# FFT convolution: the second half of the second tile's pixels loaded behind ScalarE's first copy

## The chip, the cores and the metric

The kernel runs on one core of one Trainium2 chip. The metric is the device time of one execution in microseconds, as the median of several runs. A separate profiled execution gives the trace that the views below come from.

## The reference

The reference is a circular 7x7 convolution, written as a product of two-dimensional Fourier transforms over height and width:

```
Xf = rfft2(x, axes=(1, 2))            # x: 1 x 224 x 224 x 96
Wf = rfft2(pad(w to 224 x 224))       # w: 7 x 7 x 96 x 96
Yf = einsum('bhwi,hwio->bhwo', Xf, Wf)
y  = irfft2(Yf, axes=(1, 2))          # bf16, 1 x 224 x 224 x 96
```

## The kernel before

The kernel transforms along the height only. The 224 rows are eight blocks of 28 rows; each block with 6 rows of overlap is taken to 17 frequencies (numbered s). Along the width the convolution stays direct, with the even and the odd columns combined so that fewer products are needed.

The width is cut into seven tiles of 32 columns (numbered t). The pixels of a tile come in two halves (numbered jg): half 0 holds the upper 112 image rows and half 1 the lower 112, each with 6 rows of overlap above. `load_rows` (line 177) loads a half with two DMAs on SP's queue: 112 rows of 6 KB (672 KB), then the 6 rows of overlap (36 KB). Tile 0 lies in `x0_bufs`, all later tiles in `xn_bufs` (xn0 and xn1, one for each half). `load_x(t, jg)` (line 188) loads a half of a tile.

The work has four kinds of steps, and TensorE does the products of each:

- Pixels to frequencies: matmuls of pixel columns with the matrix Fm (in the views: MATMUL pb<-Fm,xn), copied by ScalarE or VectorE from PSUM to xf. For tile 1 these are the jobs of `f_jobs` (line 535).
- Filters to frequencies: matmuls on the loaded filters wq, copied to WF (`wide_jobs`, `prep_jobs`).
- Product rounds, `b_round(t, s, ...)` (line 589): matmuls over the 96 channels for one tile and one frequency (MATMUL pb<-WF,xf and pb<-WF,J; J holds differences of xf made by VectorE). Their sums go to yf and, every few rounds, by DMA to scr in DRAM.
- Frequencies back to pixels: scr is loaded with another layout (tt), multiplied with G and put out.

At the start SP issues all loads in one sequence (lines 210 to 217): filters, tile 0's two halves with their left borders, the second copy of the filters, then both halves of tile 1. An in-order queue carries these issues.

The product rounds of tile 0 and tile 1 are interleaved by the loop at line 848. In each round, `mid()` and `end()` call jobs of other steps between the matmuls of the round, paced by steps: a queue with `add(a, b, jobs)` is spread over steps a to b - 1, two steps a round. The jobs of tile 1's first part are added at r == 1 with steps 4 to 7, that is, in the rounds r = 2 and 3. There are eight, four for half 0 and then four for half 1. Each has eight matmuls. The middle of round 2 takes three, its end three, and the middle of round 3 two. So half 0 is first read in the middle of round 2 and half 1 at its end.

In a round at the lowest and highest frequency (`if s in REAL`, line 616), ScalarE copies the first bank of products from PSUM to a temporary tile (line 619) before the second bank's products are made. For t = s = 0 this is ScalarE's first instruction of the product rounds.

The instructions of an engine follow the order in which the program names them; a helper records most of them, so that they all have line 98 in the views.

Of the kernel before, what the change touches and what calls it, by code (L numbers as in the profile page):

```python
# [63 lines left out]
def kernel(  # L64
# [7 lines left out]
    _, H, W, C = x.shape  # L72
# [12 lines left out]
    SYNC = mybir.DependencyInfo(mybir.DependencyClass.Sync, mybir.DependencyReason.DATA)  # L85
# [19 lines left out]
    VE, SE, GE, TE, DE = (_Ordered(e) for e in (nc.vector, nc.scalar, nc.gpsimd, nc.tensor, nc.sync))  # L105
# [9 lines left out]
    def bank():  # L115
        return pools["psb"].tile([128, 512], F32, name="pb")
# [60 lines left out]
    def load_rows(xb, jg, w0, npx):  # L177
        h0 = jg * HB - PAD
        n = npx * C

        def ld(p0, p1, hh):
            return dma(xb[p0:p1, 0:n], x[0, hh:hh + (p1 - p0), w0:w0 + npx, :].rearrange("h w c -> h (w c)"))
        return ld(PAD, R, h0 + PAD), ld(0, PAD, h0 % H)

    def xbuf(t, jg):
        return (xn_bufs if t else x0_bufs)[jg]

    def load_x(t, jg):
        return load_rows(xbuf(t, jg), jg, t * 2 * TW, 2 * TW)
# [13 lines left out]
    def load_copy(p, h):  # L203
        n = (C * C, WC)[h]
        for i in range(3):
            load_w(p, 0, PW - 1, h, i * n // 3, (i + 1) * n // 3)
            if i == 1:
                load_last(p + PW - 1, h)
# [4 lines left out]
        load_rows(xh_bufs[jg], jg, W - PAD, PAD)  # L213
    load_x(0, 1)
    load_copy(K1, 1)
    for jg in range(2):
        load_x(1, jg)

    wu = cpool.tile([128, 128], BF16, name="wu")
    wur = wu[:].unsqueeze(1).to_broadcast([128, 4, 128])  # L220
# [364 lines left out]
        ]  # L585

    yf_cur = {}

    def b_round(t, s, mid, end, ydve=False, planes=()):
        xf = xf_tiles[t][0:C]  # L590
# [22 lines left out]
        b0, b1 = bank(), bank()  # L613
        merge = t < 2 and s in MERGE
        tt_ = tv_pool.tile([128, 4 * C], F32, name="tt_")
        if s in REAL:
            for part in range(2):
                conv(b0, part * C, 0, part)
            SE.copy(out=tt_[:, 0:2 * C], in_=b0[:, 0:2 * C])
            mid()  # L620
            for mi, m in enumerate((2, 1)):
                for part in range(2):
                    conv(b1, (mi * 2 + part) * C, m, part)
            VE.tensor_tensor(out=yv.rearrange("p r m o -> p m r o"),
                             in0=tt_[:, 0:2 * C].rearrange("p (r o) -> p r o", o=C).unsqueeze(1).to_broadcast([128, 2, 2, C]),
                             in1=b1[:, 0:4 * C].rearrange("p (m r o) -> p m r o", m=2, r=2), op=ALU.add)
            load["a"] += 110 + 0.9 * 192
            load["v"] += 540
            for f in planes:
                f()  # L630
            end()
        else:
            v = tv_pool.tile([128, 2, 2, C], F32, name="v")
            if merge:
                conv(b0, 2 * C, 0, 0, both=True)
                conv(b0, 2 * C, 2, 0, add=True)
                conv(b0, 3 * C, 1, 0, add=True)
                conv(b0, 0, 0, 1)
                conv(b0, C, 0, 2)
                SE.mul(out=tt_[:], in_=b0[:, 0:4 * C], mul=-0.5)  # L640
                u, pr = tt_[:, 2 * C:4 * C].rearrange("p (m o) -> p m o", m=2), tt_[:, 0:2 * C]
            else:
                for part in range(3):
                    conv(b0, part * C, 0, part)
                conv(b0, 3 * C, 2, 0)
                conv(b0, 4 * C, 1, 0)
                u = tv_pool.tile([128, 2, C], F32, name="u")
                SE.mul(out=tt_[:, 0:3 * C], in_=b0[:, 0:3 * C], mul=-0.5)
                pr = tt_[:, C:3 * C]
            if puts:  # L650
                puts.pop(0)()
            if not merge:
                VE.scalar_tensor_tensor(out=u[:], in0=b0[:, 3 * C:5 * C].rearrange("p (m o) -> p m o", m=2), scalar=-0.5,
                                        in1=tt_[:, 0:C].unsqueeze(1).to_broadcast([128, 2, C]), op0=ALU.mult, op1=ALU.add)
            mid()
            for mi, m in enumerate((2, 1)):
                for pi, part in enumerate((1, 2)):
                    conv(b1, (mi * 2 + pi) * C, m, part)
            VE.scalar_tensor_tensor(out=v.rearrange("p m r o -> p m (r o)"),
                                    in0=pr.unsqueeze(1).to_broadcast([128, 2, 2 * C]), scalar=-2.0,  # L660
                                    in1=b1[:, 0:4 * C].rearrange("p (m q) -> p m q", m=2), op0=ALU.mult, op1=ALU.add)
            def ysum(eng):
                return eng.tensor_tensor(out=yv.rearrange("p r m o -> p m r o"), in0=v[:],
                                         in1=u.unsqueeze(2).to_broadcast([128, 2, 2, C]), op=ALU.add)
            if ydve:
                ysum(VE)
            last = None
            for f in planes:
                last = f()
            if not ydve:  # L670
                y = ysum(GE)
                if len(planes) > 1:
                    tc.add_manual_dep(y.ins, last.ins.name, SYNC, reason="sum after planes")
            load["a"] += 490 if merge else 410
            load["v"] += (560 if ydve else 250 if t < 2 else 0) + (560 if merge else 900)
            end()
# [103 lines left out]
    held = [0, 0]  # L780
# [34 lines left out]
    def pace(q, k):  # L815
        a, b, jobs, n = q
        if k < a:
            return
        due = n if k >= b - 1 else -(-n * (k - a + 1) // (b - a))
        while jobs and n - len(jobs) < due:  # L820
            jobs.pop(0)()

    def fills(qs, k):
        def f():
            for q in qs:
                pace(q, k)
        return f
# [20 lines left out]
    for r in range(NS + LAG):  # L848
        if r == 0:
            for i in range(1, PGRP[0][1]):  # L850
                add(max(2 * i - 3, 0), 2 * i - 1, [diff(i)])
            for i in range(N5, REAL[1]):
                add(2 * i - 2, 2 * i, [diff(i)])
            add(0, 4, fj[1][0] + fj[1][1])
            add(8, 12, fj[2][0] + fj[2][1])
        if r == 2:
            new_xf(1, SH2[0], SH2[1])
        for p in range(3):
            if r == (1, 3, 6)[p]:
                if p:  # L860
                    new_xf(1, SH2[p], SH2[p + 1])
                else:
                    xf_tiles[1] = xf_bufs[1]
                fj = f_jobs(1, p)
                if p == 2:
                    for jg in range(2):
                        fj[jg][-1] = then_load(fj[jg][-1], 2, jg)
                add((4, 7, 12)[p], (7, 11, 15)[p], fj[0] + fj[1])
        for p in range(3):
            if r == SH2[p + 1] + 1 - (p == 2):  # L870
                new_xf(2, SH2[p], SH2[p + 1])
                fj = f_jobs(2, p)
                if p == 2:
                    for jg in range(2):
                        fj[jg][-1] = then_load(fj[jg][-1], 3, jg)
                add(2 * r, 2 * r + (8, 7, 5)[p], fj[0] + fj[1])
        if r == PGRP[-2][1] + 1:
            assert not any(q[2] for q in qs[:len(PGRP) - 1])
            wtmp_cm.__exit__(None, None, None)
            t_pool = ctx.enter_context(tc.tile_pool(name="tt", bufs=NTT, side="right"))  # L880
            t2_pool = ctx.enter_context(tc.tile_pool(name="tt2", bufs=1, side="right"))
            yo_pool = ctx.enter_context(tc.tile_pool(name="yo", bufs=2, side="right"))
            g_pool = ctx.enter_context(tc.tile_pool(name="gp", bufs=1, side="right"))
            GA = g_pool.tile([KA, 4 * B], BF16, name="GA")
            GB = g_pool.tile([128, 2, 4 * B], BF16, name="GB")
            GE.memset(GA[:], 0.0)
            GE.memset(GB[:], 0.0)
        if r == 3:
            g_fin()
        if r == NS + 3:  # L890
            queue_c(0)
        for t in range(2):
            s = r - LAG * t
            if not 0 <= s < NS:
                continue
            now = bursts.pop((r, t), ())
            now = jit(*now) if now else []
            now, rest = rest + now[:2], now[2:]
            both = LAG <= r < NS
            b_round(t, s, fills(qs, 2 * r + (t if both else 0)), fills(qs, 2 * r + (t if both else 1)), False, now)  # L900
    assert not rest and not bursts and nburst == 2 * len(JGB)
    if NP2:
        ps0_cm.__exit__(None, None, None)
# [109 lines left out]
```

## Time and profile before

| what | value |
|---|---|
| median of 3 runs | 268.43 us (266.54 to 268.81) |
| profiled execution: its own time | 267.37 us |
| its span (first to last instruction) | 265.7 us |
| mean granted clock of TensorE | 0.995 |
| busy: TensorE matmuls | 252.3 us |
| busy: VectorE | 216.2 us |
| busy: ScalarE | 198.1 us |
| busy: GpSimd | 98.5 us |
| moved by DMA | 46.78 MB, mean 176 GB/s |

PE is TensorE's matmul side and PEld its weight loads, which overlap the matmuls. DVE is VectorE, ACT ScalarE, POOL GpSimd, and SPq the queue on which SyncE issues DMAs. The busy times are sums over the whole span; they tell which engine is close to the span but not where a wait lies. Times in a timeline are counted from the start of the span. In a timeline row the bracket gives how long the engine stood idle before the row and what ended that.

### The profile page before, as it was taken

To read this page: it belongs to the slowest core of one execution; us is meant where nothing else is said; L and a number is where in the kernel's file an instruction comes from. 1 tells how busy PE (TensorE), PEld (TensorE's weight loads), DVE (VectorE), ACT (ScalarE), POOL (GpSimd) and SP (SyncE) were. 2 spreads that over 40 slices of the span, in tenths; PEclk is the share of its full clock that TensorE was granted. 3 is DMA by queue.
4 is the path that set the end of the run, shared out by engine and by line. 5 is a ranking of instruction groups with operands and counts; after the bars stand their busy time and mean duration, and the time that the engine had idled before them with its cause. 6 is when DMAs were issued, how large, how long until landed. Compare 5 with 4: busy or idle time off the path is not lost.

```text
span 265.7 us, 12114 instructions
## 1 busy us (share of the span) xinstructions
PE 252.3 (95%) x5121; PEld 234.6 (88%) x5121; DVE 216.2 (81%) x459; ACT 198.1 (75%) x475; POOL 98.5 (37%) x152
## 2 busy tenths in 40 slices
PE   7987999999999999999999999999999999999993
PEld 2976999999999999999999998989999889879861
DVE  6887999899999689778887788878888889978523
ACT  8987978688854678988988799976987764287123
POOL 7782234645556442322223413333124323432100
PEclk9999999999999999999999999999999999999998
DMA  7994104511111797978785587989588533897846
GB/s 181 276 187 114 47 4 143 171 47 47 49 48 73 211 245 180 294 221 243 230 215 181 143 247 213 243 229 352 188 155 240 175 122 129 201 246 192 247 122 192
DMA packets 46946, 46.78 MB, mean 176 GB/s; under 512 B 35356, under 2 KB 38120, under 8 KB 46892
## 3 DMA queue, kind: packets, MB, share of 16 engines
q1 hardware_dynamic: 44604, 43.95, 59.3%
q10 hardware_dynamic: 2288, 2.06, 2.4%
q8 instruction: 40, 0.66, 1.1%
q14 instruction: 14, 0.11, 0.1%
HBM read 24.66 MB, written 21.33 MB: 173 GB/s over the span
## 4 chain that ended last, share of the span: by engine, by line
PE 73%; DMA 13%; DVE 8%; issue 2%; ACT 1%; SPq 1%; ACTq 0%; DVEq 0%
PE pb L98 72%; DVE J L98 3%; DMA WF<-in_x_dram 3%; DMA xf<-scra 2%; DMA tt<-scr 2%; DVE v L98 2%; DVE WF L98 2%; DMA wq<-in_w_dram 2%; DMA scrb<-yf 1%; DMA scra<-yf 1%; DMA xf<-scrb 1%; SPq L98 1%; DVE yf L98 1%; DVE u L98 1%; PE ps L98 1%
## 5 line engine op out<-in xcount | busy, mean ns | idle before, releaser
L98 PE MATMUL pb<-WF,J 96*128 96x96 bf16 x2821 | 163.0, 206 | 1.9 <-DVE J L98 1.3
L98 PEld LDWEIGHTS <-J 96*128 96x128 bf16 x2821 | 138.1, 98 | 12.6 <-issue 3.9
L98 POOL TENSOR_TENSOR yf<-v,u 128x384 bf16<-128x384 f32 x79 | 81.6, 1045 | 143.7 <-issue 85.5
L98 ACT CAST xf<-pb 96x408 bf16<-96x408 f32 (+4 forms) x140 | 65.8, 489 | 7.8 <-PE pb L98 4.4
L98 PE MATMUL pb<-WF,xf 96*128 96x96 bf16 x952 | 60.0, 206 | 0.9 <-DVE J L98 0.9
L98 DVE TENSOR_TENSOR J<-xf 96x456 bf16<-96x456 bf16 (+3 forms) x85 | 56.3, 702 | 0.0
L98 PEld LDWEIGHTS <-xf 96*128 96x128 bf16 x952 | 47.2, 98 | 1.1 <-ACT xf L98 0.8
L98 PE MATMUL pb<-Fm,xn 118*128 118x136 bf16 (+3 forms) x640 | 45.5, 199 | 1.9 <-issue 1.8
L98 PE MATMUL pb<-tt,Gm 102*84 102x384 bf16 (+1 forms) x132 | 32.8, 326 | 0.7 <-DVE u L98 0.4
L98 PEld LDWEIGHTS <-xn 118*128 118x128 bf16 x640 | 30.2, 97 | 2.2 <-issue 2.2
L98 ACT CAST J<-pb 84x384 bf16<-84x384 f32 (+1 forms) x65 | 28.0, 489 | 2.6 <-PE pb L98 2.3
L98 ACT CAST yo<-pb 84x384 bf16<-84x384 f32 (+1 forms) x63 | 27.1, 486 | 2.3 <-POOL yf L98 1.3
L98 DVE TENSOR_TENSOR J<-J 96x912 bf16<-96x912 bf16 (+2 forms) x42 | 24.1, 573 | 0.0
L98 ACT CAST WF<-pb 96x480 bf16<-96x480 f32 x42 | 21.1, 561 | 0.3 <-PE pb L98 0.3
L98 PEld LDWEIGHTS <-wq 128*128 128x128 bf16 (+1 forms) x288 | 19.7, 149 | 1.5 <-ACT wq L98 1.5
L98 DVE TENSOR_TENSOR yf<-v,u 128x384 bf16<-128x384 f32 x26 | 14.9, 572 | 0.9
L98 PE MATMUL pb<-wq 128*128 128x120 bf16 x192 | 15.2, 224 | 0.0
L98 DVE TENSOR_TENSOR WF<-WF 96x960 bf16<-96x960 bf16 x15 | 13.6, 905 | 1.4 <-ACT WF L98 1.3
L98 PEld LDWEIGHTS <-Gm 102*84 102x84 bf16 (+1 forms) x132 | 11.1, 117 | 1.0 <-issue 0.3
L98 ACT COPY xf<-xf 96x816 bf16<-96x816 bf16 (+3 forms) x20 | 11.1, 607 | 0.0
L98 PEld LDWEIGHTS <-wu 128*112 128x112 bf16 (+1 forms) x52 | 6.5, 127 | 4.8 <-issue 1.7
L98 ACT CAST tt<-pb 112x384 bf16<-112x384 f32 x8 | 3.6, 480 | 9.2 <-PE pb L98 9.0
(397 smaller groups left out, 255.7 us busy)
## 6 DMA issues: line engine op xcount, KB each, us to landing
scr<-yf SPq DMA_DIRECT2D x30, 288.0 KB
xn<-in_x_dram SPq DMA_DIRECT2D x12, 672.0 KB
tt<-scr SPq DMA_DIRECT2D x24, 336.0 KB
out_dram<-yo SPq DMA_DIRECT2D x12, 252.0 KB
out_dram<-J SPq DMA_DIRECT2D x12, 252.0 KB
tt<-scr SPq DMA_DIRECT2D x6, 288.0 KB
WF<-in_x_dram SPq DMA_DIRECT2D x2, 672.0 KB
out_dram<-tt SPq DMA_DIRECT2D x8, 168.0 KB
```

Source lines behind the costliest of these rows:

```text
L98: r = fn(*a, **k)
```

## The change

Half 1 of tile 1 is no longer issued at the start. Its two DMAs are issued after the first product round has been written down in the program, and the first of them gets a dependency on the copy that ScalarE makes in that round. SP's queue keeps the same order of DMAs, as nothing else is issued on it in between; the first of the two now waits on a semaphore of ScalarE. No other engine's order changes.

```
-    for jg in range(2):
-        load_x(1, jg)
+    load_x(1, 0)
...
+    held_x = None
...
-            SE.copy(out=tt_[:, 0:2 * C], in_=b0[:, 0:2 * C])
+            held = SE.copy(out=tt_[:, 0:2 * C], in_=b0[:, 0:2 * C])
+            if t == s == 0:
+                nonlocal held_x
+                held_x = held
...
             b_round(t, s, fills(qs, 2 * r + (t if both else 0)), fills(qs, 2 * r + (t if both else 1)), False, now)
+            if r == 0:
+                for d in load_x(1, 1):
+                    tc.add_manual_dep(d.ins, held_x.ins.name, SYNC, reason="second half behind the first products")
```

## The prediction

> **What bounds the kernel now.** I read the page first: parts 1 and 4 for the engine that sets the end, part 3 for what the queues carry.
>
> ```profile
> span 265.7 us, 12114 instructions
> PE 252.3 (95%) x5121; PEld 234.6 (88%) x5121; DVE 216.2 (81%) x459; ACT 198.1 (75%) x475; POOL 98.5 (37%) x152
> ...
> q1 hardware_dynamic: 44604, 43.95, 59.3%
> ...
> q8 instruction: 40, 0.66, 1.1%
> ...
> PE 73%; DMA 13%; DVE 8%; issue 2%; ACT 1%; SPq 1%; ACTq 0%; DVEq 0%
> ```
>
> TensorE is busy for 95% of the span and carries 73% of the chain. Time is saved or lost only where PE stands still. Queue q8 is of use below: 40 packets and 0.66 MB are 16 KB each, and PE runs 5121 + 5121 = 10242 instructions, 256 for each packet. I read q8 as PE's instruction refill.
>
> Second, the timeline of PE around the tile whose load is moved (start, length, instructions, and in brackets the idle time before).
>
> ```profile
> 21.79 0.94 PE L98 MATMUL pb<-wq 128*128 128x120 bf16 x12
> 22.89 0.39 PE L98 MATMUL pb<-Fm,xn 118*128 118x64 bf16 x8 [0.16 <-ACT xf L98]
> 25.08 0.64 PE L98 MATMUL pb<-Fm,xn 118*128 118x64 bf16 x16 [1.79 <-issue]
> 25.55 0.76 PE L98 MATMUL pb<-WF,J 96*128 96x96 bf16 x14
> 26.15 0.66 PE L98 MATMUL pb<-wq 128*128 128x120 bf16 x8
> 26.65 0.86 PE L98 MATMUL pb<-Fm,xn 118*128 118x64 bf16 x24
> ```
>
> The 1.79 us is the longest idle time of PE after its start-up. "issue" means that no semaphore ended it, and the weight load that leads the group (25.07, 1.91 us idle) waits for none. The first 8 + 16 of these matmuls read xn0 (first half), and so do 8 of the 24 at 26.65; the first one on xn1 (second half) starts at 26.88.
>
> Third, the timelines of SP's queue and of ScalarE.
>
> ```profile
> 9.42 2.63 SPq L98 DMA_DIRECT2D wq<-in_w_dram  x5
> 12.10 4.04 SPq L98 DMA_DIRECT2D xn<-in_x_dram  x4
> 28.33 0.36 SPq L98 DMA_DIRECT2D scr<-yf  x1
> ...
> 17.57 0.32 ACT L98 COPY tt__482<-pb 128x192 f32<-128x192 f32 x1 [0.64 <-PE pb L98]
> ```
>
> The four xn issues stand at 12.10 and 13.47 (first half: 112 rows, then 6), 13.98 and 15.87 (second). Nothing else is issued until 28.33. The copy that the second half will wait for ends at 17.89.
>
> Fourth, the DMA view, cut at 15.5 to 22.4, at 22.4 to 23.7, and at 24.8 to 26.1.
>
> ```profile
> DMA packets 296, 1.44 MB, mean 209 GB/s; under 512 B 54, under 2 KB 62, under 8 KB 296
> q1 hardware_dynamic: 296, 1.44, 99.3%
> ...
> q8 instruction: 1, 0.02, 5.6%
> ...
> DMA packets 0, 0.00 MB, mean 0 GB/s; under 512 B 0, under 2 KB 0, under 8 KB 0
> ```
>
> The 16 DMA engines are full of loads up to 22.4 with no refill among them. The refill then comes (22.45 to 23.62 in the trace), PE has stopped just after it began, and PE resumes at 25.07, 1.46 us after it ended. Counting PE's records, the stop is at record 705; 256 records earlier PE was at 17.99. The 37 refills from 30.45 on start from 0.7 us before to 2.8 us after PE reaches the like count, and the one in the other loaded stretch (13.91) 3.1 us after. This one starts 4.5 us after, the latest of all. I conclude that PE ran out of instructions because its refill stood behind pixel loads. This is inferred, since no row names the waiter.
>
> **The change, part by part.**
>
> *Taken away: the second half's two transfers from behind the first half.* The refill's DMA engine had to carry xn0 and xn1 rows first. The large transfer has 112 rows, 7 on each of 16 engines. From 18 to 19 us the DMA view counts 42 packets at 99.4% of 16 engines, 0.38 us each; 7 rows are 2.7 us. After the refill's end only one row packet and a few 4-byte packets follow, so the xn1 rows ran ahead of it. Without them it starts at about 22.45 - 2.7 = 19.8, ends 1.16 later at 20.9 and is of use 1.46 later at 22.4, when PE needs it at 23.1. The stall of 1.79 us goes. Bounds: 0 (the refill starts at 22.45 as now) and 1.79. I take 1.79, because the refill is asked for near 18.0 or earlier, and xn1's packets come at 18.8 (next step).
>
> *Added: one semaphore wait on SP.* SP resumes within 0.03 us of a release (scr<-yf: GpSimd's sum ends at 28.30, the issue starts at 28.33). So the 112 rows are issued at 17.92 instead of 13.98, the 6 rows at about 18.3 instead of 15.87. The scr<-yf issue's first packet comes 0.87 us after 28.33, hence 18.8 for xn1. Queued behind the waiting instruction on SP are only its own 6 rows and, next, that put at 28.33: 10 us of cover. POOL, ACT and DVE issue no DMA here and pass nothing. Who waits for xn1 is PE, at its first weight load from it. If SP's cover were gone, the puts of the products would move by the same wait, but they have readers (tt<-scr) only from 93 us on.
>
> *Moved: the landing of xn1.* The DMA engines are full without it until at least 19.0 (xn0's first semaphore update of 16 is at 20.04, and updates come about 1.1 us after the last packet). So xn1's packets arrive at 18.8 before any engine runs dry, and the same bytes end at the same time. By the trace's semaphore updates xn1 landed at 24.81 (112 rows) and 25.85 (6 rows), the last of these behind another refill (q14, 23.97 to 24.69). I take 25.2 to 25.9. Below: 24.8, with no refill in the way. Above: the full delay of the issue, 24.81 + 3.9 = 28.75.
>
> *What is late next.* Without the stall PE would reach its first xn1 matmul at 26.88 - 1.79 = 25.09. It then waits for xn1: it starts about 0.1 us after the landing, at 25.3 to 26.0. VectorE (idle 1.48) and ScalarE (idle 1.29) waited for PE in the same hole and move with it. The gain is 26.88 - 25.3 to 26.0 = 0.9 to 1.6 us; I take 1.2. Nothing behind gives it back: from 25.08 to 48.79 the chain is PE alone, and the holes later (VectorE at 49 to 55 and 74 to 79) are fed by the same PE.
>
> *Sum.* Against the profiled execution (267.37 us; span 265.7 and 1.7 around it) the changed kernel takes 266.2. That execution lies 1.06 below the median of the runs, 268.43. The measured time is a median of such runs, so I set 268.43 - 1.2 = 267.2.
>
> [...]
>
> **The rivals.**
>
> 1. *The stall stays.* Either it is not the refill, or xn1's packets get ahead of it still (18.8 against an arrival that I only place near 18). For it: no row names the waiter, and 1.46 us lie between the packet's end and PE's start. Against it: the block arithmetic and the latest start of all 39. PE then has its xn1 as now, at 26.88. No change: 268.4.
> 2. *The stall is longer in ordinary runs.* The median lies 1.06 above the profiled run. If that excess is this same start-up hole and xn1 lands by 25.1, the change saves 1.79 + 1.06 = 2.85: 265.6. For it: PE-bound work later has little reason to vary. Against it: xn1 probably lands after 25.1, and no trace of a slow run is here.
> 3. *Slower: xn1 arrives late.* If its packets are not absorbed behind xn0 and the whole delay of the issue shows, it lands at 28.75 and PE's first xn1 matmul moves from 26.88 to 28.85: +2.0, 270.4. It decides from a landing of 26.8 on. Over 1% needs a landing after 29.5. Against it: the DMA engines are 99.3% busy to 22.4, so there is a queue to join.
>
> **How the numbers follow.** Chances: forecast 0.53, first rival 0.20, second 0.15, third 0.12. One per cent (2.7 us) is about what a measurement of this kernel can tell from no change. Faster by over 1%: the second rival, 0.15, and 0.11 of the forecast, whose ordinary runs may hold part of that excess; 0.26. Slower by over 1%: 0.08, most of the third with a landing still later or a slow median. Within 1%: 0.66. The range reaches from the second rival (265.6, less 0.3) to half of the third, 265.3 to 269.4; as cases of both signs matter little, the forecast's own range is 266.8 to 267.5, from gains of 0.9 to 1.6.
>
> **What would show it.** Right: a q8 packet starting near 20 us, no "issue" hole on PE before its second group of xn matmuls, and a shorter wait for the DMA of xn before the third group. Rival 1: the hole of about 1.8 us is still at 23.3. Rival 3: PE's first xn1 matmul after 26.9, waiting for the DMA of xn. The forecast is wrong if the refill still starts after 21, or if xn1 lands after 26.8.

## The result, and the profile after

| kernel | median of 22 runs, us | smallest to largest |
|---|---|---|
| before | 268.78 | 266.44 to 270.3 |
| changed | 267.22 | 265.15 to 270.0 |

The ratio of the changed kernel to the one before is 0.994, with a 95% interval of 0.9916 to 0.9965. That is a gain of 1.6 us (0.9 to 2.3) where 1.2 was forecast. The profiled execution took 266.56 us, against 267.37 before. The page of the changed kernel:

```profile
span 264.8 us, 12115 instructions
...
PE 252.8 (95%) x5121; PEld 234.8 (89%) x5121; DVE 216.0 (82%) x459; ACT 198.0 (75%) x475; POOL 97.8 (37%) x152
...
q8 instruction: 40, 0.66, 1.1%
...
PE 72%; DMA 12%; DVE 9%; issue 2%; SPq 2%; ACT 1%; DVEq 0%; ACTq 0%
```

The totals hardly tell the two kernels apart: the same 10242 instructions of PE in the same 40 refill packets, and PE still carries the chain. The difference stands in one place, in the timeline of PE (start, length, instructions; the bracket is the idle time before):

```profile
22.16 0.94 PE L98 MATMUL pb<-wq 128*128 128x120 bf16 x12
23.00 0.86 PE L98 MATMUL pb<-Fm,xn 118*128 118x64 bf16 x24
23.70 0.76 PE L98 MATMUL pb<-WF,J 96*128 96x96 bf16 x14
24.29 0.66 PE L98 MATMUL pb<-wq 128*128 128x120 bf16 x8
24.79 0.40 PE L98 MATMUL pb<-Fm,xn 118*128 118x64 bf16 x8
25.49 0.63 PE L98 MATMUL pb<-Fm,xn 118*128 118x64 bf16 x16 [0.30 <-DMA xn<-in_x_dram]
```

The 24 matmuls on xn0 at 23.00 now run as one group, where before 8 of them were followed by 1.79 us of "issue". The later group of 24 has come apart instead: 8 still on xn0, then 0.30 us of waiting for the DMA of xn, then the first 16 on xn1. In the views of before that first matmul on xn1 stands at 26.88, here at 25.49.

The timeline of SP's queue shows the moved issues, and the DMA view from 19.6 to 21.0 shows the refill:

```profile
12.41 6.57 SPq L98 DMA_DIRECT2D xn<-in_x_dram  x4
26.90 0.36 SPq L98 DMA_DIRECT2D scr<-yf  x1
```

```profile
DMA packets 64, 0.33 MB, mean 236 GB/s; under 512 B 12, under 2 KB 12, under 8 KB 63
...
q1 hardware_dynamic: 63, 0.31, 93.4%
q8 instruction: 1, 0.02, 5.6%
```

Four xn issues still form one row, but the row now lasts 6.57 us instead of 4.04, because the last two stand at 18.28 and 18.64 (before: 13.98 and 15.87). The refill's one packet runs from 19.66 to 20.91, in the middle of the row packets. Before, it ran from 22.45, behind them.

How much of this reaches the end? I compare the start of the same matmul group in both traces. At 54.66 before it stands at 53.27 after; 79.33 becomes 77.91; 177.98 becomes 176.56; 210.89 becomes 209.46. That is 1.39 to 1.43 us, kept over 150 us. The spans differ by only 0.9. From the last of these points to the end, before took 54.8 us and the changed kernel 55.4. In the executions below, all but one with a hole of its own there (e2), this last stretch took 54.0 to 55.7; the kernel before itself took 54.8 and 54.0. So 0.6 us is of the size of the scatter there. That the change has no part in it is not shown: the three traces of the changed kernel took 55.1 to 55.7 in this stretch, more than either trace of before.

### The profile page after: what moved, and what is told of

Its sections match the earlier page's. It is cut to its first block, busy times and chain, and to the rows that moved or that the text cites. A ratio compares the mean times of both kernels' runs of the same rounds, so it can differ in the third digit from the quotient of the medians.

```text
span 264.8 us, 12115 instructions
## 1 busy us (share of the span) xinstructions
PE 252.8 (95%) x5121; PEld 234.8 (89%) x5121; DVE 216.0 (82%) x459; ACT 198.0 (75%) x475; POOL 97.8 (37%) x152
## 3 DMA queue, kind: packets, MB, share of 16 engines
HBM read 24.66 MB, written 21.33 MB: 174 GB/s over the span
## 4 chain that ended last, share of the span: by engine, by line
PE 72%; DMA 12%; DVE 9%; issue 2%; SPq 2%; ACT 1%; DVEq 0%; ACTq 0%
PE pb L98 72%; DVE J L98 3%; DMA tt<-scr 3%; DMA WF<-in_x_dram 3%; DMA xn<-in_x_dram 3%; DVE v L98 2%; DMA wq<-in_w_dram 2%; SPq L98 2%; DMA scrb<-yf 2%; DMA xf<-scrb 1%; DVE WF L98 1%; DVE yf L98 1%; DVE u L98 1%; PE ps L98 1%; DVE tt L98 0%
## 5 line engine op out<-in xcount | busy, mean ns | idle before, releaser
L98 ACT CAST yo<-pb 84x384 bf16<-84x384 f32 (+1 forms) x63 | 27.1, 486 | 2.3 <-PE pb L98 2.3
L98 PEld LDWEIGHTS <-wq 128*128 128x128 bf16 (+1 forms) x288 | 19.6, 148 | 1.4 <-issue 1.4
```

The costliest lines, as they stand in the source:

```text
L98: r = fn(*a, **k)
```

## Experiments

The theory is this one: PE runs dry because a 16 KB refill of its instructions stands in the DMA engines behind pixel rows of xn1, and the change lets the refill pass. The rivals are that the hole is something else (a semaphore, or an effect of where the code stands), that xn1's late arrival costs as much as it brings, and that the gain comes from a different place. In the diffs, "-" is the changed kernel where none is named, "+" the experiment.

### Does PE stop at a place in the code or at a number of instructions?

e3 puts 64 more PE instructions ahead of the first product, in the kernel before; e4 does the same in the changed kernel. Four of the 16 warm-up matmuls become 36 narrow ones, 32 more matmuls, each with a weight load. The result of the computation isn't touched.

```
-    warm(8)
+    pw8 = psum_tile()
+    warm(4, pw8)
+    for _ in range(36):
+        TE.matmul(pw8[:, 0, 0:32], lhsT=wu[:, 0:128], rhs=wu[:, 0:32], start=True, stop=True)
```

> The kernel before, with 4 of the 16 warm-up matmuls at the start replaced by 36 matmuls of 32 columns: 32 more matmuls with their weight loads, 64 more instructions on PE, and about the same time. Refill theory: PE runs dry at the same count of its instructions, so 64 instructions earlier in the program: not before the second group of xn matmuls, but inside round 2's first products, after 3 of the 8 matmuls pb<-WF,xf, near 21.3 us. The refill starts as in before (22 to 23, behind xn1), so the hole grows from 1.8 to about 3.7 us and ends near 25.1. Ratio 1.005 to 1.014. Rival (the hole belongs to the xn matmuls or to what they read): it stays where it was, before the second group of xn matmuls, with its 1.8 us; ratio 1.000.

> The changed kernel with the same 64 more instructions on PE. Refill theory: the refill starts at 19 to 20.5 as in the changed kernel and is of use at about 22.5, but PE is dry near 21.3, after 3 of the 8 matmuls pb<-WF,xf of round 2: a hole of about 1.1 us there (0.5 to 1.7). No hole at the second group of xn matmuls. Ratio to before 0.995 to 1.001. Rival: no hole, ratio 0.994.

Timeline of PE in e3, the padded kernel before:

```profile
21.68 0.33 PE L98 MATMUL pb<-WF,xf 96*128 96x96 bf16 x4
25.99 0.48 PE L98 MATMUL pb<-WF,xf 96*128 96x96 bf16 x4 [3.97 <-issue]
26.27 0.76 PE L98 MATMUL pb<-WF,J 96*128 96x96 bf16 x7
26.83 1.40 PE L98 MATMUL pb<-wq 128*128 128x120 bf16 x12
```

Timeline of PE in e4, the padded changed kernel:

```profile
21.41 0.33 PE L98 MATMUL pb<-WF,xf 96*128 96x96 bf16 x4
22.62 0.33 PE L98 MATMUL pb<-WF,xf 96*128 96x96 bf16 x4 [0.87 <-DVE J L98]
22.78 0.46 PE L98 MATMUL pb<-WF,J 96*128 96x96 bf16 x7
```

PE stops inside a group of eight equal matmuls, after its fourth (I had expected the third). In both kernels the stop has moved from the xn group to this place, 64 instructions earlier in the program; counted from the start it is the same 705th record. The fifth matmul does name a semaphore, one that VectorE counts up, but that wait was long met. In the kernel before and in the changed one the same matmul starts without a stop at 21.33 and 21.69, where the 39th count falls within 0.01 us of its start and the 40th comes 1.0 us later, so it needs 39 at most. In e3 there were 39 by 21.86, in e4 by 21.59, and PE went on only at 25.99 and 22.62. The "DVE J" in e4's bracket is the 40th count, which fell next to the restart; the first weight load behind the stop shows 0.98 us idle as "issue". e4 settles a second point. There the refill came early (19.56 to 20.81) and PE still went dry, because it needed those instructions 64 earlier. So the early refill of the changed kernel has little to spare.

The times are 270.46 us (ratio to before 1.0088, 1.0048 to 1.0128) for e3 and 266.69 us (0.9956, 0.9926 to 0.9986) for e4. The padding costs the kernel before 2.4 us (0.0088 of 267.63, 1.3 to 3.4 by the interval), and its hole is longer by 2.2. The execution of the trace, at 272.0 the slowest of five, lost more: 4.15 us up to the first later point of comparison, beside the hole in 6.83 us at half the granted clock, from 24.77 on (0.50 of full speed over 26.0 to 29.5). The changed kernel lost hardly anything (0.9946 without the padding on the same chip, e5 below).

### Is it enough that xn1 waits?

In e1 xn1 waits as well, but for an earlier event, ScalarE's first evacuation of half 1 of tile 0. It is issued at 16.05 instead of 18.28. In e8 the event is the last evacuation of the first filters, which gives 17.06.

```
+            r = apart(("W", 0), ob, evac(wv.rearrange("i q (b k) -> i q b k", b=2), pi, NB0 * ncol))
+            if ob == C // NB0 - 1:
+                for d in load_x(1, 1):
+                    tc.add_manual_dep(d.ins, r.ins.name, SYNC, reason="second half behind the head")
...
-            if r == 0:
-                for d in load_x(1, 1):
-                    tc.add_manual_dep(d.ins, held_x.ins.name, SYNC, reason="second half behind the first products")
```

This is e8; the lines that hold the copy's instruction go too. e1 has the same lines after the evacuation of half 1 in `head_x`.

> The second half waits for ScalarE's first evacuation of tile 0's half 1, which ends at 15.5 us in the trace of before; so its packets arrive near 16.4 (issue plus 0.87), after the filters and xn0 but before PE asks for its refill (about 17 to 18). Refill theory: the q8 packet starts at 22 to 23 as in before, PE has a hole of 1.5 to 2 us with no semaphore before its second group of xn matmuls, and the time is that of before, ratio 0.998 to 1.002. Rival (it counts only that the two issues and their waits are out of SP's start-up sequence, or that less DMA load runs beside the head's work): the hole is gone as in the changed kernel, ratio 0.994.

> The second half waits for ScalarE's last filter evacuation of the head, which ends at 16.93 us in the trace of before; its packets arrive near 17.8, just about when PE's refill reaches its DMA engine. Refill theory: either the hole (refill at 22 to 23) or none (refill at 19 to 20.5), and the time goes with it, ratio 1.00 or 0.994; which of the two tells on what side of 17.8 the refill arrives. Rival (out of the start-up sequence is what counts): no hole, 0.994, and a smooth change between the run that waits to 15.5 and this one.

The refill came at 23.19 in e1 and at 21.90 in e8, and the hole at the 705th record was back, 1.76 and 1.43 us. The times equal the kernel before: 269.37 us (1.0027, 0.9985 to 1.0069) and 268.87 us (1.0015, 0.9973 to 1.0057). The wait alone brings nothing; what counts is on which side of the refill xn1's packets come. Timeline of PE in e1, after its hole:

```profile
25.75 0.76 PE L98 MATMUL pb<-Fm,xn 118*128 118x64 bf16 x16 [1.76 <-issue]
26.32 1.31 PE L98 MATMUL pb<-WF,J 96*128 96x96 bf16 x14
```

The 14 matmuls take 1.31 us instead of 0.76. The stretches of e1 and then of before say why (stretch, its length, busy time of each engine with its instructions, granted clock of PE, DMA share, GB/s):

```profile
26.00:29.50 3.50, 3.50 (x60) 3.50 (x57) 2.52 (x4) 2.01 (x4) 1.20 (x1) 0.52 0.02 5
```

```profile
26.00:29.50 3.50, 3.50 (x88) 3.48 (x85) 3.28 (x5) 3.23 (x9) 1.32 (x1) 1.00 0.10 40
```

The granted clock over this stretch was 0.52 of full speed in e1 and 1.00 in before; in e1 it was one half from 26.12 on, for 3.41 us. From the first product to the first later point of comparison e1 needed 39.23 us and before 37.68. The waits ahead of the two xn groups add up to 2.10 us in e1 (0.34 and 1.76) and 1.95 in before (0.16 and 1.79). So the half clock cost about 1.4 us in this execution, nearly as much as the hole itself. The other runs need not have it: e1's ratio has room for 1.4 us more than before (1.0052) as well as for none.

### How late may xn1 come?

e2 ties xn1 to the multiplication that takes the copy's place in the second round (issue at 19.98), e9 to that of the third (23.71).

```
-                SE.mul(out=tt_[:, 0:3 * C], in_=b0[:, 0:3 * C], mul=-0.5)
+                held = SE.mul(out=tt_[:, 0:3 * C], in_=b0[:, 0:3 * C], mul=-0.5)
+                if t == 0 and s == 1:
+                    nonlocal held_x
+                    held_x = held
...
-            if r == 0:
+            if r == 1:
```

This is e2, where the tie to the copy goes too; in e9 the condition is s == 2 and the load follows at once.

> The second half waits for ScalarE's copy of the second round (r = 1), which ends at 20.17 in before; packets near 21.1 to 21.4, when the DMA engines have about run dry of xn0. Refill theory: refill at 19 to 20.5, no hole. The transfer alone on the engines takes about 1.8 us (0.69 MB at the 393 GB/s that the profile shows at its best), so it lands at 24.3 to 25.0, no later than in the changed kernel (25.35): PE's first xn1 matmul at 25.1 to 25.6, time equal to the changed kernel, ratio 0.992 to 0.996. Late-landing rival: the whole 2.5 us of later issue shows, landing near 27.8, ratio about 1.003.

> The second half waits for ScalarE's copy of the third round (r = 2), which ends at 23.4 in the changed kernel. Refill theory: no hole from the refill (19 to 20.5), but now the load is late: packets at 24.3, landing at 27.1 to 27.6, PE waits 1.8 to 2.3 us for the DMA of xn before its first xn1 matmul. The gain of the change is used up: ratio 0.998 to 1.004. If PE's position did not set the end here, it would stay at 0.994.

In e2 the refill passed (19.51) and the 705th record brought no hole. xn1 was issued 1.7 us later than in the changed kernel. Its 112 rows landed at 25.27 (24.61 there, 24.34 in e5), its last row at 25.50 (25.35, and 25.47 in e5), and PE waited 0.97 us for it. So most of the delay doesn't show in the last landing. It was not that the rows joined a full queue: in the two halves of the stretch from 20.0 to 21.0 the 16 DMA engines were busy for 0.39 and 0.44 of the time in e2, against 1.10 and 0.89, as good as full, in the changed kernel. The time, 267.52 us (0.999, 0.9953 to 1.0027), missed what I expected (0.992 to 0.996). The execution of the trace, the slowest of ten, has two holes far from the change. One is 1.67 us at 231.4 for the DMA of tt, followed by 3.41 us at half clock (0.57 of full speed over 232.5 to 236.5). The other stands at 100:

```profile
97.91 0.59 PE L98 MATMUL pb<-WF,J 96*128 96x96 bf16 x10
100.02 0.34 PE L98 MATMUL pb<-WF,J 96*128 96x96 bf16 x4 [1.53 <-issue]
```

It is the same kind of stop at another place. PE stops behind record 4289, which is 705 + 14 x 256. The refill packet for what follows ran from 97.04 to 98.40 (in before from 95.13 to 96.22), and PE went on 1.62 us after its end. The loads of tt run at this place: in before, where they are issued from 93.09 on, the 16 DMA engines were busy for 0.99 of the time from 93 to 95 and 1.20 from 95 to 97, as good as full; in e2 it was 0.67 from 98 to 103. Whether the late issue brings these holes about stays open; e2's time decides nothing.

e9 shows the third rival's mechanism:

```profile
24.98 0.40 PE L98 MATMUL pb<-Fm,xn 118*128 118x64 bf16 x8
29.15 0.63 PE L98 MATMUL pb<-Fm,xn 118*128 118x64 bf16 x16 [3.77 <-DMA xn<-in_x_dram]
...
30.16 0.76 PE L98 MATMUL pb<-WF,J 96*128 96x96 bf16 x7
```

PE waits 3.77 us for xn1, which landed at 29.01; I had expected 27.1 to 27.6. The x7 row at 0.76 us (0.46 elsewhere) shows the half clock after it, for 3.41 us. The time is 271.55 us (1.012, 1.008 to 1.0161). The ratio lies above what I had expected (0.998 to 1.004). So there is a point from which holding back costs a wait of several us: between an issue at 20.0 (e2) and one at 23.7.

### The same two kernels again

e5 and e11 are the changed kernel without an edit, e6 the kernel before.

> The changed kernel once more, on the same chip as the others of this group and for a second trace: ratio 0.992 to 0.997, no hole at the second group of xn matmuls, PE at the check points (its idle times before pb<-WF,J near 53, 78 and 83 us) 1.2 to 1.6 us earlier than in before. In the first trace 0.6 us of that was lost behind 228 us in waits for transfers; if that belongs to one execution and not to the change, this trace loses another amount there.

> The kernel before once more, for a second trace of it: ratio 0.997 to 1.003. Refill theory: again a q8 packet at 22 to 23.5, PE dry at its 705th record, a hole of 1.5 to 2.0 us before the second group of xn matmuls; in some executions followed by 3.4 us at half the granted clock, as after the same hole in the run that waited to 15.5.

> The changed kernel beside the split one on the same chip, with a third trace: ratio 0.992 to 0.997; no refill hole; a wait for xn of 0.2 to 1.1 us, ending 0.1 to 0.2 us after its last row lands; product rounds 1.0 to 1.8 us earlier than in before at the check points up to 210 us.

e5 repeated the result: refill at 19.58, no hole, 266.32 us (0.9946, 0.992 to 0.9973). But PE waited 1.02 us for xn1 where the first trace had 0.30. e6, before against itself, gave 1.0035 (0.9998 to 1.0072): a comparison here has an error of about 0.35%, so ratios are read to that. Its trace had the late refill (22.09) and a hole of 1.50 at the 705th record again. That execution took 265.98 us, less than the changed kernel's first trace without a hole (266.56): single executions scatter by more than the gain, and only the medians tell it.

e11 was the surprise. Its time is 267.1 us (0.9976, 0.9948 to 1.0003), and its timeline of PE looks like that of before:

```profile
18.47 0.46 PE L98 MATMUL pb<-WF,J 96*128 96x96 bf16 x7 [0.16 <-issue]
...
23.00 0.40 PE L98 MATMUL pb<-Fm,xn 118*128 118x64 bf16 x8
24.89 0.64 PE L98 MATMUL pb<-Fm,xn 118*128 118x64 bf16 x16 [1.50 <-DVE WF L98]
```

Its DMA view from 19.6 to 21.0 has no line of q8, where the first trace of the changed kernel had one:

```profile
DMA packets 66, 0.34 MB, mean 241 GB/s; under 512 B 11, under 2 KB 11, under 8 KB 66
...
q1 hardware_dynamic: 66, 0.34, 99.1%
```

The bracket names VectorE, but the weight load that leads the group waits for no semaphore. The refill came at 22.33, behind xn1. I see the reason one refill earlier: that one ended at 16.95, where those of the other two traces of the changed kernel ended at 15.50 and 15.62. PE stopped for it behind record 449, exactly 256 ahead of 705, and went on at 18.47. If PE asks for the next refill when it passes this place, it asked later than usual, and xn1, issued at 18.03, was ahead.

All traces beside each other (times in us; the issue is that of the 112 rows; the last column counts from the first product, so that the start-up, which varies by 0.9 us, falls out):

| kernel | issue of xn1 | previous refill ends | this refill starts | hole at record 705 | first xn1 matmul, from the first product |
|---|---|---|---|---|---|
| before | 13.98 | 15.43 | 22.45 | 1.79 | 9.90 |
| before again (e6) | 13.95 | 15.66 | 22.09 | 1.50 | 9.40 |
| e1 | 16.05 | 15.98 | 23.19 | 1.76 | 11.15, half clock |
| e8 | 17.06 | 16.51 | 21.90 | 1.43 | 9.22 |
| changed, third trace (e11) | 18.03 | 16.95 | 22.33 | 1.50 | 9.59 |
| changed | 18.28 | 15.62 | 19.66 | none | 8.14 |
| changed again (e5) | 17.66 | 15.50 | 19.58 | none | 8.88 |
| e2 | 19.98 | 15.53 | 19.51 | none | 8.86 |
| e9 | 23.71 | 16.08 | 20.24 | none | 11.55 |
| e7 | 17.86 | 15.53 | 19.70 | none | 9.16 |
| e10 | 17.74 | 15.29 | 19.72 | none | 8.01 |
| e12 | 20.49 | 15.58 | 19.60 | none | 7.71 |

Two groups stand apart: this refill starts at 19.5 to 20.2 with no hole, or at 21.9 to 23.2 with one. Two columns sort them: with the issue 2.16 us or more behind the end of the previous refill the refill passes, with 1.08 or less it does not. The padded kernels fit too: e3 issues 1.40 behind (14.49 against 13.09) and loses, e4 3.11 behind (18.17 against 15.06) and wins. Another measure sorts all 14 traces as well, the issue against PE's first record after the 449th: the refill passes where xn1 is issued at most 0.12 us ahead of that record (18.28 against 18.40 in the changed kernel) and fails from 0.44 ahead on (18.03 against 18.47 in e11). Which of the two counts these runs can't tell. It is a race. With the changed kernel's release it was won in five of six traces (two of the changed kernel's three, e7, e10 and e4); how often in runs without a trace isn't known. When PE asks for a refill no row tells; that part is inferred.

### Can it be bettered?

The remaining cost in the changed kernel is the wait for xn1. e7 issues its 6 rows at the start and holds back only the 112 (in the changed kernel's code both transfers get the dependency, not the first alone). e10 splits xn1 by columns, the 17 pixels that are read first in front:

```
-                for d in load_x(1, 1):
+                xb, w1 = xn_bufs[1], 2 * TW
+                split = []
+                for c0, c1 in ((0, 17), (17, 2 * TW)):
+                    for p0, p1, hh in ((PAD, R, HB), (0, PAD, HB - PAD)):
+                        split.append(dma(xb[p0:p1, c0 * C:c1 * C], x[0, hh:hh + (p1 - p0), w1 + c0:w1 + c1, :].rearrange("h w c -> h (w c)")))
+                for d in split:
```

e12 is e10 tied to the second round, as in e2. The edit of e7:

```
+    dma(xn_bufs[1][0:PAD, 0:XW], x[0, HB - PAD:HB, 2 * TW:4 * TW, :].rearrange("h w c -> h (w c)"))
...
-                for d in load_x(1, 1):
+                d = dma(xn_bufs[1][PAD:R, 0:XW], x[0, HB:2 * HB, 2 * TW:4 * TW, :].rearrange("h w c -> h (w c)"))
+                if True:
```

> The changed kernel, but of the second half only the 112 rows wait for the copy; its 6 rows are issued at the start, behind the first half. In the changed kernel PE waited 0.30 us for the 6 rows (landed 25.35; the 112 rows 24.61). Expected: the refill stays at 19 to 20.5, PE's wait for xn falls to 0 to 0.15 us, first xn1 matmul at 25.1 to 25.3; ratio to before 0.991 to 0.996, 0.001 better than the changed kernel at most. If the refill falls behind the 6 rows and more, a hole of up to 1 us comes back.

> The changed kernel, but the second half comes as two pieces by columns: 17 pixels of all rows first (what the first two jobs read), then the other 15. After the refill, what is left in this place is PE's wait for the last row of xn1 (0.30 and 1.02 us in the two traces of the changed kernel). With half the bytes ahead of the first use, the first piece should land 0.8 to 1.2 us earlier and the wait go to 0 to 0.2. Expected: no refill hole, first xn1 matmul 8.1 us after the first product (8.14 and 8.88 in the changed kernel), ratio to before 0.990 to 0.996, equal to the changed kernel or up to 0.003 better. Against it: two more DMAs with more, smaller packets, and the next refills on the same DMA engine may hold up the piece as well; then the wait stays.

> The split by columns together with the wait for round 1's copy. In the third trace of the changed kernel the refill was late again (22.33) and the hole came back: there the refill before it ended at 16.95 instead of 15.6, so this one was asked for late, and xn1's packets (issue 18.03) were first. Race theory: with the issue near 20.0 the refill wins in any execution (start 19 to 20.5), as it did in the run that waited to round 1. The first piece then lands at 23.6 to 24.4, PE needs it at 24.5: a wait of 0 to 0.2 us. First xn1 matmul 7.9 to 8.2 us after the first product; ratio to before 0.988 to 0.995. If the race does not matter for the median, it equals the split run (0.991).

e7 missed: the wait was 0.63, not 0 to 0.15, and the time 266.91 us (0.9968, 0.9941 to 0.9995). The 112 rows themselves landed late, at 25.95, beside two refills (q14 at 24.41 to 24.77, q8 at 24.53 to 25.64). In this trace the six rows, landed by 23.53, are not what PE waited for. It also waited 0.56 us at 23.24 for the last rows of xn0.

e10 took the wait away. Its timeline of PE:

```profile
22.77 0.86 PE L98 MATMUL pb<-Fm,xn 118*128 118x64 bf16 x24
23.47 0.76 PE L98 MATMUL pb<-WF,J 96*128 96x96 bf16 x14
24.07 0.68 PE L98 MATMUL pb<-wq 128*128 128x120 bf16 x8
24.59 0.86 PE L98 MATMUL pb<-Fm,xn 118*128 118x64 bf16 x24
```

Both groups of 24 run whole, without a bracket. The time is 267.06 us (0.9911, 0.9867 to 0.9954). e12 combines this with an issue 4.9 us behind the previous refill, well on the winning side, and has the earliest first xn1 matmul of all (7.71 from the first product); its time is 267.28 us (0.9946, 0.9907 to 0.9985). Both beat the kernel before. Neither is shown to beat the changed kernel, whose own intervals (0.9916 to 0.9965, 0.992 to 0.9973 and, in e11, 0.9948 to 1.0003) overlap with theirs: what is left to win there, 0.3 to 1.0 us, is of the size of the comparison's error.

## Why the prediction was right, point by point

- *The stall is the refill behind xn1's rows, and it goes.* Right, in mechanism and place. What was inferred is now shown: the stop moves with the instruction count (e3, e4), comes back with the late refill (e1, e8, e11), is absent with the early one where the count is not moved, and stands at other places too when the refill there is late, 256 records ahead of 705 (449 in e11) and 14 times 256 behind it (4289 in e2). So the block arithmetic of the prediction, 256 records for each refill packet, holds. One refill 2.8 us late (22.45 against 19.66) left PE dry, and in e11 PE stopped at two block ends in succession (449 and 705). The refill was forecast for 19.8 to 20.9 and ran from 19.66 to 20.91.
- *Of use 1.46 us after its end.* About right. In six traces that ran dry at the refill's place PE resumed 1.22 to 1.48 us after the packet ended, in e4 1.81; at the two other places it was 1.52 (e11) and 1.62 (e2). Why e4 took longer isn't known.
- *The added wait.* Forecast: issues at 17.92 and 18.3. Found: 18.28 and 18.64 in an execution whose first product came 0.37 us later (17.35 against 16.98), so the same. Nothing behind it on SP's queue was touched: the put of yf went from 28.33 to 26.90, with PE.
- *xn1 lands at 25.2 to 25.9.* Right in the time of each span: 24.61 for the 112 rows and 25.35 for the 6, 25.47 in e5. With the later first product taken out, 25.35 stands for 24.98 on the time of before, a little earlier than forecast. In this kernel a later issue moved the last landing little, up to e2's 19.98; e9 shows the end of that.
- *PE waits for xn1, first xn1 matmul at 25.3 to 26.0.* Right: 25.49, after 0.30 us of waiting, 25.61 after 1.02 in e5. Between the two kernels' first traces the gain is 1.39 us, within the forecast 0.9 to 1.6; counted from the first product it is 1.76, and 1.02 with e5.
- *Nothing behind gives it back.* Right as far as the last points of comparison, at 210 us. Behind them it stays open: the traces of the changed kernel need 0.3 to 1.8 us longer there than those of before.
- *The sum, 267.2.* Measured 267.22, and that this is so close is luck. The forecast took 1.2 from a median of three runs, 268.43. Over 22 runs the kernel before has 268.78, and the gain is 1.6; the two differences, 0.35 and 0.4, cancel.
- *Rival 1, the stall stays.* It lost as a description of the kernel and holds for single executions. Its words "xn1's packets get ahead of it still" are what e11 shows, one of three traces of the changed kernel. The prediction treated the two arrivals (18.8 and "near 18") as fixed points; they vary, the one with the release of the copy and the other with the end of the previous refill.
- *Rival 2, a longer stall in ordinary runs.* Not shown, not excluded. The half clock after the hole (about 1.4 us in e1) is a way in which ordinary runs of before could lose more than its trace, and the prediction had no such term. Its condition, xn1 landing by 25.1, held in the first trace by a little (24.98 on the time of before) and not in e5 (25.47, or 25.72 on that time). From the traces of the stretch alone the changed kernel would gain 1.2 us where the race is won and nothing where it is lost (first later point at 37.68 and 37.16 after the first product before, 35.92 and 36.58 changed, 37.44 in e11); the measured 1.6, with 0.9 to 2.3 around it, has room for 1.2 and for more. How many runs go at half clock can't be read from times without traces; that stays open.
- *Rival 3, xn1 late.* Real as a mechanism (e9), which needed an issue 5.4 us later than the changed kernel's.

## What to carry to other kernels

An idle time that the profile puts down to "issue", on a weight load without a wait, may be instructions that are not there yet, as the 1.79 us of the kernel before were: count the engine's instructions, divide by the refill packets (here 10242 by 40, 256 for each), and look where the packets of the instruction queue ran. Loads that are needed later than the next refill belong behind it. Here one dependency did that, at the price of a wait of 0.30 to 1.02 us for the load itself. Such an order is a race unless it has slack: look at several traces, and choose a release with a margin on both sides.

## What the runs showed of the hardware that was not expected

- A refill waited behind data: with the rows of xn1 issued early it started 1.7 to 3.7 us later (21.9 to 23.2 against 19.5 to 20.2), in a kernel whose refill packets take 1.1% of the span of the DMA engines. In e2 one more was late, at 97.04 (95.13 in before), at the place of the loads of tt.
- Holes of PE of 1.76 (e1), 1.67 (e2) and 3.77 us (e9) were followed by half the granted clock, for 3.41 us; in e3, whose hole is 3.97 us long, it began inside the hole and lasted 6.83 us. The measured clock was 0.52 over 26.0 to 29.5 in e1, 0.57 over 232.5 to 236.5 in e2 and 0.50 over 26.0 to 29.5 in e3. Holes of 1.79 (before), 1.53 (e2, at 100), 1.50 (e6 and e11) and 1.43 us (e8) were not followed by it. In e1 PE stood idle for 2.1 of the 3.41 us before the half clock (1.76 and 0.34). Why one hole of 1.76 us is followed by it and another of 1.79 is not, no run here shows.
- The last rows of a load landed by up to 0.7 us apart in the same kernel (8.00 and 8.74 us after the first product, with 0.30 and 1.02 us of waiting, in two traces of the changed one), next to refills on q14 at about 24 us (24.07 to 24.52 in the first trace). Which row shares an engine with which refill was not followed further.
